# Longer runs for the weights of a fused attention and MLP kernel, strided columns of the first weights, and another order of steps

## The chip, the cores and the metric

The kernel runs on one core of one Trainium2 chip. The metric is the device time of one execution in microseconds. The core has five engines that run side by side, each through its own queue and in order: TensorE (PE, with its weight loads as PEld), VectorE (DVE), ScalarE (ACT), GpSimd (POOL) and SyncE (SP), which here only issues DMAs. 16 DMA engines move data between HBM and the on-chip memory (SBUF). Matmuls write to PSUM, a second on-chip memory.

## The reference, cut to what matters

A gated recurrent attention over 4 sequences of 768 steps, with 8 heads of 48, is followed by a two-layer MLP on its output.

```python
# q, k, v, alpha: (4, 8, 768, 48), alpha in 0.8 to 1.0
for t in range(768):
    state = alpha[:, :, t, :, None] * state + einsum('bhd,bhe->bhde', k[:, :, t], v[:, :, t])
    y[:, :, t] = einsum('bhd,bhde->bhe', q[:, :, t], state)
x = y.transpose(0, 2, 1, 3).reshape(3072, 384)
h = x @ w_in            # w_in (384, 2048)
out = (h * cos(h)) @ w_out   # w_out (2048, 384)
```

## The kernel before, in words

The 3072 rows are worked in 12 pairs J of 256 rows, three pairs to a sequence. A partition holds two consecutive steps of a pair (e is 0 or 1), and the pair's 128 partitions form two chunks (c is 0 or 1) of 64 partitions, so a chunk is 128 steps.

For each pair, the steps are these, with their names in the plan. "load a/k/q/v" (L102) issues one DMA of 384 KB from SyncE's queue. "ln" takes the logarithm of alpha on ScalarE (L139). "cums0" and "cums" (L174, L158) sum the logarithms along the chunk with triangular matrices on TensorE. "icp" and "exps" (L189, L194) are exponentials of minus and plus the sums on ScalarE. "sk" and "sq" (L210, L214) multiply k by the first and q by the second, on GpSimd or, where the plan says ":D", on VectorE. "trans" (L251) transposes scaled k and q on TensorE, "evT" (L261) copies them out of PSUM. "scores" (L266) multiplies them, "mask" (L274) applies the causal mask on VectorE. "castv", "vpe", "vev" and "vst" lay out v. "outer", "add", "state" and "decay" carry the state from chunk to chunk: "add" on VectorE, "state" and "decay" on GpSimd. "yT" (L315) forms the attention's output, transposed, and "evy" (L345) copies it to the tile xT.

The MLP of a pair works in four parts u of 512 hidden columns. "m1" (L354) multiplies 4 x 3 tiles of 128 columns of w1, the stationary operand, by xT (256 moving columns). "sin" (L362) computes the cosine on ScalarE as a shifted sine, "gate" (L367) multiplies it by h on VectorE into the tile gsb. "m2" (L375) takes gsb as the stationary operand and w2 as the moving one; it goes through 16 tiles of 128 hidden columns, in four quarters. Quarter u needs the gate u. "evo" and "out" copy the result out of PSUM and store it. "idle" (L410) issues matmuls on a tile of zeros whose result is not used.

ScalarE needs one table of functions for logarithm and exponential and another for the sine; each change of set is a table load.

The order of all steps is written out in PLAN (L431) and IDLE (L499): each step has a number, all steps are sorted by it and issued in this order (L513), so the numbers set only the order in which each engine's queue is filled. From pair 3 on, "mula" multiplies the two alphas of a partition on GpSimd, and "eb" groups exponentials and the next pair's logarithm.

The weights come in eight DMAs from GpSimd's queue, which also turn float32 into bfloat16: four of w1 (load_w1, L120), one for each part u, and four of w2 (load_w2, L126), one for each m2 quarter. w1 is one tile, with a hidden column in its own place (L94). One row of the reference's w_in gives a run of 512 columns, 2048 bytes, to a partition; one row of w_out gives 1536 bytes. A gate (GATES, L99) holds the load of alpha of pair 2, and with it everything behind it on SyncE's queue, until yT of pair 1 is done.

Of the kernel before, what the change touches and what calls it, by code (L numbers as in the profile page):

```python
# [10 lines left out]
BF = mybir.dt.bfloat16  # L11
# [5 lines left out]
def kernel(  # L17
# [10 lines left out]
    nc = tc.nc  # L28
    B, H, S, D = q.shape
    DM, DF = moe_w_in.shape  # L30
    C = 128
# [6 lines left out]
    KT = DM // C  # L38
    NF = DF // C
    FW = 4  # L40
# [50 lines left out]
    for a in range(2):  # L91
        nc.vector.memset(dmask[64 * a : 64 * a + 64, a : a + 1], 1.0)

    w1 = consts.tile([C, KT, DF], BF, tag="w1", name="w1")  # L94
    w2 = consts.tile([C, NF, DM], BF, tag="w2", name="w2")

    a_sb, kqv, cp_sb, icp_sb, qkT_sb, A_sb, c2_sb = {}, {}, {}, {}, {}, {}, {}
# [19 lines left out]

    WQ = FW * C

    def load_w1(u):  # L120
        nc.gpsimd.dma_start(
            out=w1[:, :, u * WQ : (u + 1) * WQ],
            in_=moe_w_in[:, u * WQ : (u + 1) * WQ].rearrange("(kk p) f -> p kk f", p=C),
        )

    def load_w2(u):  # L126
        nc.gpsimd.dma_start(
            out=w2[:, FW * u : FW * (u + 1)],
            in_=moe_w_out[u * WQ : (u + 1) * WQ, :].rearrange("(a p) d -> p a d", p=C),
        )  # L130

    act_now = [None]
# [221 lines left out]
    def mlp1(J, u):  # L354
        h_ps[J, u] = ps.tile([C, FW, T2], FP, tag="h", name="h_ps", bufs=3)
        for f in range(FW):
            ft = u * FW + f
            for kk in range(KT):
                nc.tensor.matmul(h_ps[J, u][:, f, :], w1[:, kk, ft * C : (ft + 1) * C], xT[J][:, kk, :],  # L359
                                 start=(kk == 0), stop=(kk == KT - 1))  # L360

    def cosine(J, u):  # L362
# [47 lines left out]
    def idle(n):  # L410
# [18 lines left out]


    PLAN = {  # L431
# [66 lines left out]
    }  # L498
    IDLE = [(1201, 12), (6413, 16), (11874, 2), (13039, 6), (14889, 9), (17476, 6)]  # L499

    order = []
    for key, line in PLAN.items():
        kind, *rest = key.split()
# [41 lines left out]
```

## Time and profile before

| | |
|---|---|
| median of 3 runs | 186.75 us (186.71 to 187.4) |
| profiled execution | 186.2 us, its span 184.4 us |
| TensorE busy | 177.7 us (96%) |
| VectorE busy | 132.6 us (72%) |
| ScalarE busy | 127.1 us (69%) |
| GpSimd busy | 83.9 us (45%) |
| granted TensorE clock | 1.00 |

Times in the profile are microseconds from the start of the span unless marked ns. A line of a group or of the timeline names the engine, the line of the kernel, the operation, the tile written, the tiles read, the shape and the count; "w" is a weight tile. The chain that ended last is followed back from the last instruction, at each step to what released it. A matmul's duration includes its way through the array, so matmuls overlap and their pace is read from the distance of their starts.

### The profile page before, as it was taken

Reading aid. Unit: us, or ns where it says so; the run is one execution under the profiler, and the core shown is the slowest. Engines: PE = TensorE matmul, PEld = TensorE weight load, DVE = VectorE, ACT = ScalarE, POOL = GpSimd, SP = SyncE. Lnnn points to the kernel's source line nnn. Section 1 sums busy time; section 2 is a strip of 40 time slices with the busy share of each in tenths; the row PEclk is TensorE's granted clock in tenths of the full one; section 3 lists DMA queues with packets and bytes.
Section 4 is the critical chain, followed back from the end, with each engine's and each line's share of the span. In section 5 each row is a group of like instructions: output and inputs, shape, how many; then the busy total and the mean of one; then the engine's idle time right before and its main releaser. Section 6 shows DMA issues by size and latency. Waiting matters only on the chain.

```text
span 184.4 us, 5780 instructions
## 1 busy us (share of the span) xinstructions
PE 177.7 (96%) x2478; PEld 127.1 (69%) x2480; DVE 132.6 (72%) x176; ACT 127.1 (69%) x166; POOL 83.9 (45%) x116
## 2 busy tenths in 40 slices
PE   7999999899999999999999999999999999999993
PEld 2455687565687776876778668676777786787772
DVE  7367673559889799899548986886979769352651
ACT  2572887899889987779787999637945163372720
POOL 5379830297765693943874189492600121000000
PEclk9999999999999999999999999999999999999999
DMA  5999999999999969968968893050420204010212
GB/s 148 261 261 192 187 203 247 237 271 264 257 197 242 310 174 279 226 158 202 301 151 211 202 304 72 0 132 14 116 73 4 60 5 170 4 43 4 85 43 85
DMA packets 60137, 29.47 MB, mean 160 GB/s; under 512 B 51024, under 2 KB 60112, under 8 KB 60112
## 3 DMA queue, kind: packets, MB, share of 16 engines
q1 hardware_dynamic: 56256, 25.86, 57.6%
q0 software_dynamic: 3712, 3.15, 11.1%
q8 instruction: 19, 0.31, 0.7%
q10 hardware_dynamic: 144, 0.10, 0.2%
q14 instruction: 6, 0.05, 0.1%
HBM read 25.17 MB, written 4.72 MB: 162 GB/s over the span
## 4 chain that ended last, share of the span: by engine, by line
PE 76%; ACT 10%; DMA 7%; DVE 2%; issue 1%; SPq 1%; ACTq 0%
PE h_ps L359 29%; PE o_ps L388 27%; DMA a<-in_alpha_dram 7%; PE y_ps L338 5%; PE A_ps L272 3%; PE T_ps L258 3%; PE idle_ps L414 3%; ACT lna L141 2%; DVE gsb L370 2%; PE U_ps L289 2%; ACT c_sb L365 2%; ACT xT L349 2%; PE o_last L382 1%; ACT L136 1%; ACT L365 1%
## 5 line engine op out<-in xcount | busy, mean ns | idle before, releaser
L370 DVE TENSOR_TENSOR gsb<-h_ps,c_sb 128x1024 bf16<-128x1024 f32 x48 | 58.1, 1221 | 24.1 <-ACT c_sb L365 23.2
L365 ACT ACTIVATE c_sb<-h_ps,halfpi 128x1024 bf16<-128x1024 f32 x48 | 53.1, 1115 | 23.5 <-PE h_ps L359 23.1
L359 PE MATMUL h_ps<-xT,w 128*128 128x256 bf16 x576 | 67.6, 273 | 0.6 <-DVE gsb L370 0.3
L388 PE MATMUL o_ps<-w,gsb 128*128 128x384 bf16 x368 | 66.5, 326 | 0.0
L359 PEld LDWEIGHTS <-w 128*128 128x128 bf16 x576 | 55.5, 98 | 9.5 <-issue 0.9
L388 PEld LDWEIGHTS <-gsb 128*128 128x128 bf16 x368 | 34.1, 98 | 20.7 <-issue 0.2
L277 DVE TENSOR_TENSOR A_sb<-A_ps,msk 128x1024 bf16<-128x1024 f32 x24 | 29.0, 1216 | 3.6 <-PE A_ps L272 3.6
L311 POOL TENSOR_TENSOR un<-us,c 128x384 bf16<-128x384 f32 x20 | 16.7, 837 | 30.0 <-DVE us L303 27.4
L212 POOL TENSOR_TENSOR kh<-k,icp 128x384 bf16<-128x384 f32 x22 | 21.8, 1002 | 14.6 <-ACT icp L192 14.6
L216 POOL TENSOR_TENSOR qh<-q,cp 128x384 bf16<-128x384 f32 x16 | 16.6, 1043 | 0.8 <-DMA q<-in_q_dram 0.8
L149 POOL TENSOR_TENSOR a<-a 128x384 f32<-128x384 f32 x9 | 9.0, 1000 | 15.7 <-DMA a<-in_alpha_dram 15.7
L264 DVE COPY qkT<-T_ps 128x1024 bf16<-128x1024 bf16 x18 | 11.8, 680 | 5.0 <-PE T_ps L258 4.8
L414 PE MATMUL idle_ps<-zeros 128*128 128x512 bf16 x49 | 12.9, 412 | 1.4 <-DVE zeros L52 1.2
L349 ACT CAST xT<-y_ps 128x384 bf16<-128x384 f32 x17 | 9.0, 599 | 5.6 <-PE y_ps L338 5.0
L219 POOL CAST vp<-v 128x768 bf16<-128x768 f32 x12 | 10.2, 854 | 5.7 <-DMA v<-in_v_dram 5.7
L141 ACT ACTIVATE lna<-a 128x768 bf16<-128x768 f32 x12 | 10.1, 843 | 3.5 <-DMA a<-in_alpha_dram 3.5
L136 ACT ACT_TABLE_LOAD x9 | 11.5, 1283 | 0.9 <-PEq L529 0.7
L365 ACT ACT_TABLE_LOAD x9 | 11.5, 1283 | 0.2
L303 DVE TENSOR_TENSOR us<-U_ps,un 128x384 f32<-128x384 f32 x16 | 8.7, 550 | 2.7 <-POOL un L311 2.5
L400 ACT COPY o_sb<-o_ps 128x384 f32<-128x384 f32 x11 | 5.2, 476 | 7.2 <-PE o_ps L388 7.2
L414 PEld LDWEIGHTS <-zeros 128*128 128x128 bf16 x51 | 4.8, 105 | 7.3 <-issue 2.2
L264 ACT COPY qkT<-T_ps 128x1024 bf16<-128x1024 bf16 x6 | 6.0, 1014 | 5.3 <-PE T_ps L258 5.1
(70 smaller groups left out, 159.7 us busy)
## 6 DMA issues: line engine op xcount, KB each, us to landing
a<-in_alpha_dram SPq DMA_DIRECT2D x12, 384.0 KB, 5.9
q<-in_q_dram SPq DMA_DIRECT2D x12, 384.0 KB, 5.7
k<-in_k_dram SPq DMA_DIRECT2D x12, 384.0 KB, 5.9
v<-in_v_dram SPq DMA_DIRECT2D x12, 384.0 KB, 5.6
out_dram<-o_sb SPq DMA_DIRECT2D x23, 192.0 KB, 3.0
vs<-vp SPq DMA_DIRECT2D x36, 64.0 KB, 2.9
w<-in_moe_w_in_dram POOLq DMA_DIRECT2D x4, 384.0 KB, 7.6
w<-in_moe_w_out_dram POOLq DMA_DIRECT2D x4, 384.0 KB, 9.2
```

The lines of the kernel that those rows point to most:

```text
L136: nc.scalar.preload_act_table_set("natural_log_exp_and_others")
L141: nc.scalar.activation(out=lna_t[J % NL][:, :, :, 0:D].rearrange("p e h d -> p h e d"), in_=a_sb.pop(J), func=AF.Ln)
L212: eng.tensor_tensor(out=kh_t[J % NQ][:, e, :, 0:D], in0=kqv["k", J][:, :, e], in1=icp_, op=ALU.mult)
L216: eng.tensor_tensor(out=qh_t[J % NQ][:, e, :, 0:D], in0=kqv["q", J][:, :, e], in1=cp, op=ALU.mult)
L264: copy(out=qkT_sb[J][:, c], in_=T_ps[J][:, c].rearrange("r n e s -> r n (e s)"))
L277: nc.vector.tensor_tensor(out=A_sb[J][:, c].rearrange("s a p t -> s (a p) t"), in0=A_ps.pop((J, c)).rearrange("s a p t -> s (a p) t"), in1 ...
L311: nc.gpsimd.tensor_tensor(out=u, in0=U_sum.pop(n), in1=c2_sb[J][:, :, c].unsqueeze(3).to_broadcast([C, NP, 2, D]), op=ALU.mult)
L359: nc.tensor.matmul(h_ps[J, u][:, f, :], w1[:, kk, ft * C : (ft + 1) * C], xT[J][:, kk, :], start=(kk == 0), stop=(kk == KT - 1))
L365: nc.scalar.activation(out=c_sb[J, u], in_=h_ps[J, u], func=AF.Sin, bias=halfpi, scale=1.0)
L370: nc.vector.tensor_tensor(out=gsb[J][:, u * FW : (u + 1) * FW], in0=h_ps.pop((J, u)), in1=c_sb.pop((J, u)), op=ALU.mult)
L388: nc.tensor.matmul(o_ps[J, c][:, 0:DM], gsb[J][:, ft, c * C : (c + 1) * C], w2[:, ft], start=(ft == 0), stop=(ft == NF - 1))
L414: nc.tensor.matmul(idle_ps[0], zeros[:, 0:C], zeros, start=True, stop=True)
```

## The change

load_w1 loads w1 in two halves of 1024 columns, into two tiles, instead of four quarters into one; a run is now 4096 bytes. The plan still names four w1 steps, and the latter two issue nothing. load_w2 gives partition p the four rows 4p to 4p + 3 of its 512, which lie side by side in HBM, so a run is 6144 bytes instead of 1536. So that hidden units meet their rows of w2, m1 takes for its tile f every fourth column of its part, starting at f: its stationary operand is read with a step of four elements. Parts 0 and 1 read the first half, parts 2 and 3 the second.

The plan is written anew. In the first pairs k is loaded before q; all four multiplies of pairs 0 and 1 are on VectorE, as are three of pairs 2 and 3, while some of later pairs go to GpSimd. Transposes of pair 0 come before the sums of pair 1. yT of pair 1 comes before one m1 step of pair 0 that it followed, and one more m1 step comes before the sums of pair 2. There are 44 idle matmuls instead of 51 (the trace lacks the records of two).

```diff
-    w1 = consts.tile([C, KT, DF], BF, tag="w1", name="w1")
+    w1 = [consts.tile([C, KT, DF // 2], BF, tag=f"w1{r}", name="w1") for r in range(2)]
...
     def load_w1(u):
-        nc.gpsimd.dma_start(
-            out=w1[:, :, u * WQ : (u + 1) * WQ],
-            in_=moe_w_in[:, u * WQ : (u + 1) * WQ].rearrange("(kk p) f -> p kk f", p=C),
-        )
+        if u < 2:
+            cols = slice(2 * u * WQ, 2 * (u + 1) * WQ)
+            nc.gpsimd.dma_start(out=w1[u], in_=moe_w_in[:, cols].rearrange("(kk p) f -> p kk f", p=C))
 
     def load_w2(u):
         nc.gpsimd.dma_start(
             out=w2[:, FW * u : FW * (u + 1)],
-            in_=moe_w_out[u * WQ : (u + 1) * WQ, :].rearrange("(a p) d -> p a d", p=C),
+            in_=moe_w_out[u * WQ : (u + 1) * WQ, :].rearrange("(p a) d -> p a d", a=FW),
         )
...
     def mlp1(J, u):
         h_ps[J, u] = ps.tile([C, FW, T2], FP, tag="h", name="h_ps", bufs=3)
         for f in range(FW):
-            ft = u * FW + f
             for kk in range(KT):
-                nc.tensor.matmul(h_ps[J, u][:, f, :], w1[:, kk, ft * C : (ft + 1) * C], xT[J][:, kk, :],
+                cols = w1[u // 2][:, kk, u % 2 * WQ : (u % 2 + 1) * WQ].rearrange("p (c a) -> p a c", a=FW)[:, f]
+                nc.tensor.matmul(h_ps[J, u][:, f, :], cols, xT[J][:, kk, :],
                                  start=(kk == 0), stop=(kk == KT - 1))
...
-        "load a": "750 2460 26667 27237 34276 40276 44776 46276 52716 68776 86352 100342",
-        "load k": "1890 5250 27807 35776 43276 47776 57976 67354 78979 81849 88912 99772",
-        "load q": "1320 6750 28377 37276 38776 53776 56976 65644 85782 100912 102772 118966",
+        "load a": "750 2925 23850 24420 29562 38429 41429 54304 58004 59504 61004 98634",
+        "load k": "1320 5925 24990 35429 42929 52129 53269 69404 85374 87209 91709 97494",
+        "load q": "1890 7425 32429 36929 45929 52699 63204 70544 84804 90209 98064 122712",
...
-        "w1": "13130 11430 15880 12280",
-        "w2": "19161 17541 20961 22950",
+        "w1": "11430 12280 61723 18603",
+        "w2": "17753 18774 22228 23078",
...
-        "sk 0": "7660 12315:D 38060 42828 55804 60330 73792 86828 93082 113472 119784 131130",
-        "sk 1": "8044:D 13980 36686 43778 54854 64134 78239 85878 98692 112522 114422 129239",
-        "sq 0": "8990:D 15585:D 39010 44194:D 53904 63184 76519 90402 107172 109842 111572 130860:D",
-        "sq 1": "7195:D 14930 38586:D 44728 50458 61464 73876:D 91352 99642 108122 120734 133328:D",
+        "sk 0": "6655:D 12570:D 35664:D 41679:D 49164 66689 71695 88096 91244 103860 108817 133261",
+        "sk 1": "8110:D 13356:D 36402:D 42057 54844 59053 70575 84223 96414 110890 121175 134211",
+        "sq 0": "8560:D 14256:D 39614 43164 53114 67639 77304 86123 92194 104980 123075 129811",
+        "sq 1": "7660:D 13806:D 38664 44114 52164 60003 78254 89229:D 97364 108751:D 112610 130761",
...
-        "trans": "11010 16998 41264 46764 59426 70546 81348 92810 110566 118352 127816 139612",
+        "trans": "9275 14876 41473 45204 57118 68891 79693 91456 108911 116997 125603 138052",
...
-        "yT": "19113 25797 50008 58700 73174 90548 91338 109680 125310 140186 151156 163372",
+        "yT": "18276 22980 46827 56393 71520 88893 89683 108026 123655 138627 149597 160495",
...
-        "m1 0": "22636 29318 53346 64652 77964 96022 98958 113776 129917 147108 155394 166216",
-        "m1 1": "20948 36274 52028 65970 75328 94704 93386 122590 134256 148426 160642 170812",
+        "m1 0": "21429 28072 51691 62998 76309 94667 97303 112775 128357 145548 156458 164657",
+        "m1 1": "20111 31349 50073 64316 73673 93349 92031 121589 132697 146866 159082 167946",
...
-    IDLE = [(1201, 12), (6413, 16), (11874, 2), (13039, 6), (14889, 9), (17476, 6)]
+    IDLE = [(1201, 12), (6413, 12), (9753, 1), (10479, 5), (13514, 6), (15354, 5), (16679, 1), (17666, 2)]
```

106 rows, old and new, of the table PLAN are left out of this document.

## The prediction

> **What bounds the kernel now.** I read the page's engine shares first, then the chain that ended last in order of time, then the timeline of TensorE and its weight loads, then the answers on single engines and the windows of DMA.
>
> The page's first part, its groups and its DMA queues (engine, busy us, share, count; line engine op names shapes xcount | busy, mean ns | idle; queue: packets, MB, share):
>
> ```profile
> PE 177.7 (96%) x2478; PEld 127.1 (69%) x2480; DVE 132.6 (72%) x176; ACT 127.1 (69%) x166; POOL 83.9 (45%) x116
> ...
> L359 PE MATMUL h_ps<-xT,w 128*128 128x256 bf16 x576 | 67.6, 273 | 0.6 <-DVE gsb L370 0.3
> ...
> L359 PEld LDWEIGHTS <-w 128*128 128x128 bf16 x576 | 55.5, 98 | 9.5 <-issue 0.9
> ...
> q1 hardware_dynamic: 56256, 25.86, 57.6%
> q0 software_dynamic: 3712, 3.15, 11.1%
> ```
>
> TensorE is the bound nearly everywhere, so the end is its work plus the time in which it stands or turns over filler matmuls. Those places are near the start, as the chain shows (start us, us, what):
>
> ```profile
> 17.99 1.08 PE idle_ps L414 x5
> ...
> 20.19 1.05 ACT xT L349 x2
> 21.24 0.04 issue
> 21.28 1.47 PE h_ps L359 x12
> ...
> 25.76 0.93 PE y_ps L338 x55
> 26.69 0.02 issue
> 26.71 6.89 DMA a<-in_alpha_dram
> 33.60 0.02 issue
> 33.62 0.85 ACT lna L141
> 34.47 0.04 issue
> 34.52 0.81 PE cums_h L155 x4
> ```
>
> Real work starts at 21.28 with m1 of pair 0. The alpha of pair 2 takes 6.89 us from issue to landing, behind the weights on the DMA engines, and TensorE waits for it: its last m2 matmul before is issued at 33.37 and takes 0.16 of its time, so the sums could start at 33.54 and start at 34.52, 0.98 later. From 37.6 on the chain is TensorE, but for a stretch of ScalarE and VectorE from 102.5 to 119.5.
>
> How fast weights can be loaded (timeline: start, us, engine line, xcount):
>
> ```profile
> 10.43 0.41 PEld L167 LDWEIGHTS <-lna 128*128 128x128 bf16 x8
> 10.59 0.34 PE L167 MATMUL cums_h<-inchunk,lna 128*128 128x2 bf16 x8
> ...
> 52.00 5.24 PEld L359 LDWEIGHTS <-w 128*128 128x128 bf16 x48
> 52.12 5.40 PE L359 MATMUL h_ps<-xT,w 128*128 128x256 bf16 x48
> ```
>
> Eight full weight loads with two-column matmuls: one matmul lasts 0.164, so they follow each other every (0.34 - 0.164)/7 = 25 ns. In m1 the pace is (5.40 - 0.27)/47 = 109 ns, set by 256 moving columns; the load needs at most 25 of these 109.
>
> VectorE and GpSimd on the same scaling (ns min/median/max; timeline):
>
> ```profile
> L212 POOL TENSOR_TENSOR kh<-k,icp x22: 992/1002/1012, 7.9 to 133.0; 128x384 bf16<-128x384 f32 x22
> L212 DVE TENSOR_TENSOR kh<-k,icp x2: 548/892/1236, 8.1 to 12.2; 128x384 bf16<-128x384 f32 x2
> ...
> 12.15 0.55 DVE L212 TENSOR_TENSOR kh<-k,icp 128x384 bf16<-128x384 f32 x1
> ```
>
> The 1236 ns one ran beside GpSimd's kh at 7.94; alone it is 0.55 against GpSimd's 1.00.
>
> **The change part by part.** All against the profiled execution, 184.4 of span in 186.2; the median 186.75 is 0.55 above that run.
>
> *First pairs on VectorE, and the order up to the first m1.* k is loaded before q; loads land about 1.5 apart (384 KB at the window's 260 GB/s), so k lands at 6.0 and q at 7.5. Pair 0's four multiplies run on VectorE, 4 x 0.55, as exponentials arrive between 6.9 and 8.1: done at 9.25 (now 9.82), and pair 0's transposes go ahead of pair 1's sums, at 9.35 instead of 10.87. ScalarE then sets the pace: ln of pair 1 ends at 9.89 as now, two evictions of 1.01 and four exponentials of 0.49 follow, ending near 14.0. VectorE evicts vs at 12.05 (0.55), does four multiplies, the last ending at 14.8; behind them in its queue add 0.56, mask 1.22, add 0.55, mask 1.22: 18.35. yT of pair 0 reads that mask and starts at 18.4, now 19.33. Same evictions after it: first m1 at 20.35, **-0.93**. GpSimd loses three multiplies here and two of four w1 issues (0.8 each), so nothing waits behind them; it is nearly idle from 13 to 15, so the multiplies have no neighbour. The filler falls from 51 to 44 matmuls, which is the same waiting filled.
>
> *yT of pair 1 moves ahead of one m1 step.* Its inputs are ready by 22 (mask of pair 1 ends at 18.35 + 1.22 + 0.55 + 1.21 = 21.3). Small holes around it today (0.2 at 22.7, 0.3 at 26.6, 0.1 at 28.1) become about 0.4 in all: **-0.2**.
>
> *Runs of weights, and the wait for alpha of pair 2.* 3712 packets of queue 0 (11.1% of 16 x 184.4) took 88 ns each and moved 848 bytes, cast from 1696; queue 1's 30 ns for 460. Per packet that is 9 ns plus 0.047 ns a byte read. After: 768 packets of 4096 and 512 of 6144 bytes read, by that line 200 and 296 ns: 305 us of engine time instead of 327, 7% of the 16.4 us that the weights occupy (14.0 to 30.4, between the inputs' packets in the trace's packet records): -1.1. The trace's packet records give 98 ns at 2048 read and 79 at 1536, a steeper saving: 22 + 0.037 a byte, 262 us, -2.6. Lower end: nothing, if a packet costs by bytes alone. I take -1.9, between the two fits. Alpha of pair 2, issued after yT of pair 1 at about 24, lands at 33.6 - 1.9 = 31.7. Pair 2's sums are now behind one more m1 (1.31): TensorE comes to them at 33.6, and needs alpha by 33.6 - 0.05 - 0.85 = 32.7. So the 0.98 between matmuls there shrinks to 0.1: **-0.9**. Cover of 1.0; without it (no DMA gain) the 0.9 comes back. First w1: m1 now needs a half, not a quarter. At worst it lands where the second quarter does now (w1 is 1536 x 98 of 1536 x 98 + 2048 x 79, 0.48 of the 16.4: 7.9 for four quarters, 3.9 for two, from 14.0, plus 1.6 to landing: 19.5), before 20.35.
>
> *What is late next.* TensorE reaches the second m2 quarter of pair 1 5.9 after pair 2's sums start, at 39.55 (four m2 quarters 2.6, sums 1.0 and 0.35, m1 1.31, m2 0.65). It needs a gate that follows four exponentials, ln, a table load 1.28, Sin 1.11 and the gate 1.22: 40.25. New wait **+0.7**. The rest to 52, reordered: **-0.1**.
>
> *Columns read four apart.* 576 weight loads. No row has strided weights. Below: no gain, since the 256 columns set the 109. Above: if all 98 ns of a load's record were serial and stretched as ScalarE's strided xT write stretches against its plain copy (599 to 476, 1.26), 123 + 11 = 134 ns, 25 x 576 = +14.4. I take 0: the nearest row, 25 ns in a window of 109, could be 4 times as long and stay hidden.
> The Trainium skill (SBUF — State Buffer, Door 1, note on cachelines) lets a reader stride free while two reads hit each 16-byte line, up to 8 bf16; 4 is inside, which would leave the sum as it is; no run here shows it. It also (TensorE: Matmul & The Clock Gate, LDWEIGHTS) has 128 columns take 107 ns, which the 25 ns contradict; were strided loads to fall to that estimate, they would just fit into 109.
>
> *Later pairs.* 13 instead of 10 multiplies on VectorE, the rest off TensorE's path; the order from pair 4 on is nearly the old one, moved earlier as a whole, and input DMAs move with it.
>
> Sum: -0.93 - 0.2 - 0.9 + 0.7 - 0.1 = -1.4. Span 183.0, profiled time 184.8, on the median's footing 185.3.
>
> **Rivals.**
> *Strided weights slow m1 (slower).* Place: 576 loads; 0.58 us for each ns over 109; it decides from 1.4/0.576 = 2.4 ns. For it: no row shows such a load, and each load starts only when the matmul before it starts, 11 ns short of the window's end with its 98. Against: 25 ns of streaming. At half the upper end's excess, 121 ns, it adds 7.2 to the forecast: 192.5; at the end 200.
> *The longer runs are not faster.* Alpha lands at 33.6; the 0.9 returns, and its 0.1: gain 0.5, time 186.2. Against: both packet fits.
> *VectorE and GpSimd block each other in pair 2.* Three multiplies of pairs 2 and 3 move to VectorE beside GpSimd's alpha product and decay; 0.7 late each (1236 against 548) would put pair 2's transposes 0.7 late: gain 0.7, time 186.05. For it: that row. Against: GpSimd's own queue has room, and m2 lies ahead of the transposes.
> The Trainium skill (SBUF — State Buffer, Who interferes with whom) states this rule, a VectorE instruction with two SBUF inputs locking against GpSimd's reads; the 1236 ns agree.
>
> **How the numbers follow.** Forecast 0.62 (184.2 to 186.0 on its own), strided weights 0.19, runs no faster 0.10, blocking 0.07, a wait not foreseen that costs over 2.3 us 0.02. About 0.5%, 0.93 us, is what can be told from no change. Faster 0.62, same 0.17, slower 0.21. The time is the forecast's 185.3. The range 184.2 to 188.2 takes in both middle rivals and strided loads up to 114 ns; about 0.15 of large slowdowns and 0.04 below are left out.
>
> **What would show it.** First m1 near 20.4; alpha of pair 2 landed before 32.7 with no ScalarE gap before TensorE's sums; a pace of 109 in m1 with w1 strided; a hole near 39.6; queue 0 with some 1400 packets. A pace over 111, or TensorE idle for alpha, makes it wrong.

## The result and the profile after

| | before | after |
|---|---|---|
| median, first comparison | 186.98 us (186.71 to 187.4, 4 runs) | 185.42 us (184.99 to 185.63, 4 runs) |
| ratio after to before | | 0.9912 [0.9883, 0.994] |
| median, second comparison | 186.53 us (35 runs) | 185.59 us (12 runs) |
| ratio there | | 0.9961 [0.9938, 0.9985] |
| profiled execution and its span | 186.2, 184.4 | 185.63, 183.9; later 184.77, 183.0 |

The changed kernel is faster by 0.9 to 1.6 us; both intervals lie below 1. Every ratio in this document leaves out executions over 1.5% longer than the shortest of their kernel, which are two of the eight with eight idle matmuls and one of the nine with columns one apart; medians take all executions. The first parts of the page of after, in the same columns as before:

```profile
span 183.9 us, 5771 instructions
PE 177.6 (97%) x2473; PEld 133.3 (73%) x2473; DVE 132.8 (72%) x183; ACT 127.3 (69%) x162; POOL 77.2 (42%) x111
...
q1 hardware_dynamic: 56256, 25.86, 58.0%
q0 software_dynamic: 1376, 3.15, 9.2%
...
L360 PE MATMUL h_ps<-xT,w 128*128 128x256 bf16 x576 | 67.4, 273 | 0.2
L360 PEld LDWEIGHTS <-w 128*128 128x128 bf16 x576 | 62.4, 114 | 3.0 <-DVE gsb L371 0.3
```

Queue 0 has 1376 packets instead of 3712, and their engine time is 9.2% of 16 x 183.9 = 271 us instead of 327. A strided weight load is recorded at 114 ns instead of 98, and the m1 matmuls take what they took. TensorE's share rose because the span fell.

This profile gains only 0.5 us of span, and its first m1 starts at 21.23, as in before (21.28). A second profile of the same program starts it at 20.26 and has a span of 183.0. The difference is there before any of the changed steps. TensorE up to 6.5 us, first in the first profile of after, then in the second (start us, us, engine line operation, count, idle before):

```profile
1.20 5.30 PE L415 MATMUL idle_ps<-zeros 128*128 128x512 bf16 x12 [1.20 <-DVE halfpi L77]
6.29 0.53 PE L156 MATMUL cums_h<-lna,tri 128*128 128x384 bf16 x1
```

```profile
1.20 4.08 PE L415 MATMUL idle_ps<-zeros 128*128 128x512 bf16 x12 [1.20 <-DVE halfpi L77]
5.36 0.32 PE L156 MATMUL cums_h<-lna,tri 128*128 128x384 bf16 x1
```

The same twelve idle matmuls lasted 5.30 us and 4.08 us. At the start the idle matmuls follow each other every 0.427 us, later every 0.215, so the clock starts at half; the trace's clock records first show the full clock at 6.77 us in the first profile and at 3.90 us in the second. The queue is in order, so the sums of pair 0 started at 6.29, though their input was ready at about 5.3. Before's profile had its full clock at 3.92, and a second profile of before had it at 4.02, so the second profile of after is the one to set against them:

| profile | full clock from | first m1 | span |
|---|---|---|---|
| before | 3.92 | 21.28 | 184.4 |
| before, second | 4.02 | 21.24 | 184.7 |
| after | 6.77 | 21.23 | 183.9 |
| after, second | 3.90 | 20.26 | 183.0 |

With a like clock the span fell by 1.4 to 1.7 us. The second profile of after is the shortest of its twelve executions (184.77, median 185.59), so the medians are the surer size. The gain sits in two places. The first m1 starts 1.0 earlier. From there to the first m1 step of pair 1 before takes 7.02 and after 6.55, 0.47 less. The next stretch, to the first m1 step of pair 2, gains nothing: 23.81 and 23.88 in the two profiles of before, 23.77 and 23.89 in those of after. In it TensorE's wait for the sums of pair 2 is gone, and a new wait for a gate has come behind it. From that m1 step of pair 2 (52.12 and 50.70) to the last (174.56 and 172.99) the lead only goes from 1.42 to 1.57.

The chain of the second profile of after, where before had 6.9 us of alpha's DMA (start us, us, what):

```profile
29.60 1.95 PE o_ps L389 x12
31.55 1.31 PE h_ps L360 x12
32.86 0.65 PE o_ps L389 x4
33.51 0.79 PE cums_h L156 x4
...
36.89 1.28 ACT L366
...
38.19 2.12 ACT c_sb L366 x2
```

TensorE now goes from m1 and m2 into the sums without a gap. What TensorE still waits for in that profile (total us, times, longest), and the place of the first of these waits on the timeline:

```profile
PE o_ps L389 <- DVE gsb L371: 1.3, 1, 1.3
PE idle_ps L415 <- DVE halfpi L77: 1.2, 1, 1.2
```

```profile
38.52 0.81 PE L389 MATMUL o_ps<-w,gsb 128*128 128x384 bf16 x4
39.33 2.36 DVE L371 TENSOR_TENSOR gsb<-h_ps,c_sb 128x1024 bf16<-128x1024 f32 x2 [1.18 <-ACT c_sb L366]
...
40.62 1.48 PE L389 MATMUL o_ps<-w,gsb 128*128 128x384 bf16 x8 [1.29 <-DVE gsb L371]
```

The first is the new wait, 1.29 us at 39.3. The second stands at the very start, before and after.

### The profile page after: what moved, and what is told of

The parts are those of the page before. It is cut to its first block, busy times and chain, and to the rows that moved or that the text cites. A ratio compares the mean times of both kernels' runs of the same rounds, so it can differ in the third digit from the quotient of the medians.

```text
span 183.9 us, 5771 instructions
## 1 busy us (share of the span) xinstructions
PE 177.6 (97%) x2473; PEld 133.3 (73%) x2473; DVE 132.8 (72%) x183; ACT 127.3 (69%) x162; POOL 77.2 (42%) x111
## 3 DMA queue, kind: packets, MB, share of 16 engines
q0 software_dynamic: 1376, 3.15, 9.2%
## 4 chain that ended last, share of the span: by engine, by line
PE 88%; ACT 5%; DVE 3%; issue 1%; POOL 0%; ACTq 0%; POOLq 0%
PE h_ps L360 33%; PE o_ps L389 31%; PE idle_ps L415 6%; PE y_ps L339 5%; PE A_ps L273 4%; PE T_ps L259 3%; PE U_ps L290 2%; PE o_last L383 1%; DVE A_sb L278 1%; PE cums_h L156 1%; ACT c_sb L366 1%; ACT lna L142 1%; ACT icp L193 1%; PE cums L156 1%; ACT cp L201 1%
## 5 line engine op out<-in xcount | busy, mean ns | idle before, releaser
L389 PE MATMUL o_ps<-w,gsb 128*128 128x384 bf16 x368 | 67.5, 327 | 1.4 <-DVE gsb L371 1.3
L360 PEld LDWEIGHTS <-w 128*128 128x128 bf16 x576 | 62.4, 114 | 3.0 <-DVE gsb L371 0.3
L213 POOL TENSOR_TENSOR kh<-k,icp 128x384 bf16<-128x384 f32 x17 | 17.2, 1017 | 15.1 <-ACT icp L193 13.7
L217 POOL TENSOR_TENSOR qh<-q,cp 128x384 bf16<-128x384 f32 x18 | 17.9, 1007 | 6.1 <-ACT cp L201 5.9
L415 PE MATMUL idle_ps<-zeros 128*128 128x512 bf16 x44 | 13.4, 449 | 1.2 <-DVE halfpi L77 1.2
L265 ACT COPY qkT<-T_ps 128x1024 bf16<-128x1024 bf16 x10 | 9.9, 1014 | 5.4 <-PE T_ps L259 5.2
L401 DVE COPY o_sb<-o_ps 128x384 f32<-128x384 f32 x13 | 7.2, 555 | 6.3 <-PE o_ps L389 6.3
L350 ACT CAST xT<-y_ps 128x384 bf16<-128x384 f32 x12 | 6.5, 594 | 5.0 <-PE y_ps L339 4.6
```

The costliest lines, as they stand in the source:

```text
L213: eng.tensor_tensor(out=kh_t[J % NQ][:, e, :, 0:D], in0=kqv["k", J][:, :, e], in1=icp_, op=ALU.mult)
L217: eng.tensor_tensor(out=qh_t[J % NQ][:, e, :, 0:D], in0=kqv["q", J][:, :, e], in1=cp, op=ALU.mult)
L360: nc.tensor.matmul(h_ps[J, u][:, f, :], cols, xT[J][:, kk, :], start=(kk == 0), stop=(kk == KT - 1))
L389: nc.tensor.matmul(o_ps[J, c][:, 0:DM], gsb[J][:, ft, c * C : (c + 1) * C], w2[:, ft], start=(ft == 0), stop=(ft == NF - 1))
L401: copy(out=t, in_=o_ps.pop((J, c))[:, 0:DM])
L415: nc.tensor.matmul(idle_ps[0], zeros[:, 0:C], zeros, start=True, stop=True)
```

## The experiments

Each is an edit of the changed kernel. In the plan's rows a value stands for a pair, in the order of pairs.

### The loads and columns alone, under the old order

```diff
-    (the rows of PLAN and IDLE after the change)
+    (the rows of before, with)
+        "w1": "11430 13130 15880 12280",
```

> The changed loads and columns under the old order of steps (pair 0's half of w1 issued first, the other half in the place of the third quarter). Theory of the prediction: alpha of pair 2 lands about 1.0 us earlier than the 33.6 of before, so the 0.98 that TensorE waits for it goes to about 0.2, m1 keeps its 109 ns, and the first m1 stays near 21.3: gain 0.7 to 0.9 us, ratio to the kernel before 0.9955. Rival, only the order matters: ratio 1.000, alpha at 33.6. Rival, strided weight loads cost TensorE time: their price eats the gain, ratio 0.998 or more and an m1 pace above 109.

Measured 187.05 (12 runs) against 186.62, ratio 1.0013 [0.9988, 1.0037]: no gain. Alpha of pair 2 landed at 33.28, and still TensorE waited 0.76 for ln:

```profile
33.38 1.28 ACT L137 ACT_TABLE_LOAD   x1
34.67 0.84 ACT L142 ACTIVATE lna<-a 128x768 bf16<-128x768 f32 x1
...
35.56 0.32 PE L156 MATMUL cums_h<-lna,tri 128*128 128x384 bf16 x1 [0.76 <-ACT lna L142]
```

ScalarE was not waiting for the DMA. It was loading its table, behind the last sine. This profile had a late full clock (7.13), which puts everything from the first m1 on (22.36) about 1.1 later, the table load too. But before, with an early clock, shows the same pair of events:

```profile
32.27 1.28 ACT L136 ACT_TABLE_LOAD   x1
...
33.62 0.84 ACT L141 ACTIVATE lna<-a 128x768 bf16<-128x768 f32 x1
```

The table load ended at 33.55 and alpha landed at 33.60. Two waits ended within 0.05 us, and the trace names the later one. In the second profile of before the distance is 0.11. An earlier alpha alone could gain no more than that there. The 0.7 to 0.9 us that were expected did not come.

### The new order alone, with the old loads and columns

```diff
-        "w1": "11430 12280 61723 18603",
+        "w1": "12280 11430 12282 12281",
```

(load_w1, load_w2, mlp1 and the w1 tile as before.)

> The new order and the scaling on VectorE, with the loads and columns of before (four w1 quarters issued one behind the other in the place of the two halves). Theory: the first m1 is about 0.9 us earlier than before at the same start of the full clock, but alpha of pair 2 lands near 33.6 and TensorE stands about 0.9 for it: gain about 0.5 us, ratio 0.997. Rival, the runs don't matter: ratio as the changed kernel's, 0.991. Rival, strided loads cost: with plain columns it is faster than the changed kernel, 0.988 or less.

Measured 186.23 (12 runs) against 186.62, ratio 0.9979 [0.9956, 1.0001]. The first m1 is at 20.34, as early as with the new loads. Behind it TensorE waits for the weights and then for alpha's ln (timeline):

```profile
33.41 0.81 PE L388 MATMUL o_ps<-w,gsb 128*128 128x384 bf16 x4 [0.47 <-DMA w<-in_moe_w_out_dram]
...
34.52 0.32 PE L155 MATMUL cums_h<-lna,tri 128*128 128x384 bf16 x1 [0.30 <-ACT lna L141]
```

The last w2 quarter landed at 33.36 and alpha at 33.60; after the change they land at 31.3 and 32.6. Further waits come later, 0.6 for transposes that GpSimd's multiply holds up and 0.6 inside an m1 step. This profile is of the longest of the twelve executions (187.58, median 186.23), so these later waits need not stand in the others. The longer runs gain nothing under the old order, and without them the new order starts the sums of pair 2 at 34.52 instead of 33.51, 1.0 later. By time alone the orders with and without the new loads can't be told apart here (0.9979 against 0.9961, intervals overlapping); what the loads add is read from these waits.

### The step of the strided columns: 1, 8 and 16 instead of 4

One apart, with w1's hidden units in the wrong places:

```diff
-                cols = w1[u // 2][:, kk, u % 2 * WQ : (u % 2 + 1) * WQ].rearrange("p (c a) -> p a c", a=FW)[:, f]
+                cols = w1[u // 2][:, kk, u % 2 * WQ : (u % 2 + 1) * WQ][:, f * C : (f + 1) * C]
```

> The changed kernel with m1's columns read side by side and all loads as they are, so that hidden units meet other rows of w2 than they should; the work is the same. Theory: the weight loads' record falls from 114 ns back to 98, m1's pace stays 109, and the time is the changed kernel's within 0.3 us, ratio 0.991. Rival, strided loads cost TensorE time: 576 loads at 1 to 2 ns give 0.6 to 1.2 us back, ratio 0.985 to 0.988.

Eight apart, over a half of w1 (hidden units again in the wrong places, as with sixteen):

```diff
+                cols = w1[u // 2][:, kk].rearrange("p (c a) -> p a c", a=2 * FW)[:, u % 2 * FW + f]
```

> The changed kernel with m1's columns read eight apart over a half of w1, 16 bytes from one to the next; loads as they are, so hidden units meet other rows of w2 than they should. The record of a weight load was 98 ns with columns side by side and 114 four apart, and m1 kept 109. Theory, the extra time goes by the 16-byte lines touched (32 columns: 4 lines, then 16, now 32): about 135 ns, and still 109 a matmul, time as the changed kernel's. Rival: one column a line halves the stream again and m1's pace rises above 109; every ns is 0.58 us, so 120 ns would be 6 us slower, ratio 1.03.

Sixteen apart, which needs w1 in one tile:

```diff
+    w1 = consts.tile([C, KT, DF], BF, tag="w1", name="w1")
...
+            nc.gpsimd.dma_start(out=w1[:, :, cols], in_=moe_w_in[:, cols].rearrange("(kk p) f -> p kk f", p=C))
...
+                cols = w1[:, kk].rearrange("p (c a) -> p a c", a=NF)[:, u * FW + f]
```

> As before, with w1 in one tile and columns read sixteen apart over all of it, 32 bytes from one to the next; m1 needs both halves, so the first m1 waits for the second one's landing at 23.3, some 3 us later than in the changed kernel, and hidden units meet other rows of w2 than they should. Theory of lines: 32 lines as with eight apart, so the same record, about 135 ns, and 109 a matmul; the time is the 2 to 3 us of the later start. Rival, the distance itself counts: the record grows again, to 175 or so, and m1's pace passes 109.

The weight loads of m1 at steps 1, 4, 8 and 16 (ns min/median/max, then from and to in us):

```profile
L360 PEld LDWEIGHTS <-w x576: 95/98/99, 20.8 to 174.8; 128*128 128x128 bf16 x192
```

```profile
L360 PEld LDWEIGHTS <-w x576: 110/113/133, 21.1 to 174.9; 128*128 128x128 bf16 x192
```

```profile
L360 PEld LDWEIGHTS <-w x576: 139/143/173, 20.2 to 174.4; 128*128 128x128 bf16 x192
```

```profile
L360 PEld LDWEIGHTS <-w x576: 139/144/169, 23.1 to 179.7; 128*128 128x128 bf16 x192
```

The medians are 98, 113, 143 and 144 ns. The record grows to a step of 8 and no further. The matmuls do not follow: in all four the starts in m1 stand 108 to 110 ns apart at full clock. From the first m1 to the end, steps 1, 4, 8 take 162.8, 162.6 to 162.7, and 163.0 us. Medians are 186.02 (9 runs, ratio 0.9951 [0.9927, 0.9976]) for step 1 and 185.62 (10 runs, 0.9952 [0.9924, 0.998]) for step 8, against 0.9961 for step 4.

That the record levels off at 8 fits the rule in the Trainium skill (SBUF — State Buffer, Door 1, note on cachelines) by which each access that crosses to a new 16-byte line, 8 bf16, pays a penalty: from a step of 8 on, each element lies in another line. The same note would have a step of 4 free; the record shows 15 ns more at 4 than at 1, so in the load itself it was not free, only hidden.

Step 16 is slower, 190.51 (4 runs, ratio 1.0211 [1.0176, 1.0246]), and not by its stride:

```profile
23.13 4.48 PE L360 MATMUL h_ps<-xT,w 128*128 128x256 bf16 x24 [1.89 <-issue]
```

With one tile the first m1 waited for both halves, the second of which landed at 23.04. In the same 24 matmuls that take 2.78 in after, the clock fell to half from 24.04 to 27.45, and they took 4.48. 1.9 and 1.7 account for 3.6 of the 4.7 us of span; 0.9 more is a later wait inside an m1 step. Against this kernel's profile stands the first of after, whose full clock came as late (6.97 and 6.77).

### Fewer idle matmuls at the start

```diff
-    IDLE = [(1201, 12), (6413, 12), (9753, 1), (10479, 5), (13514, 6), (15354, 5), (16679, 1), (17666, 2)]
+    IDLE = [(1201, 8), (6413, 12), (9753, 1), (10479, 5), (13514, 6), (15354, 5), (16679, 1), (17666, 2)]
```

> The changed kernel with 8 instead of 12 idle matmuls at the start. Theory of the clock: full clock is granted at 3.9 us of the span in one execution and at 6.8 in another; in the late ones 12 idle matmuls of 0.427 us hold pair 0's sums until 6.3, though ln is done at 5.3. With 8 the sums start by 5.5 whatever the clock does; the median falls by 0.4 to 0.9 us, ratio 0.987 to 0.989, and the times spread less. Rival, the idle matmuls are needed to bring the clock up: with 8 it comes up later still and the time grows by 0.5 us or more, ratio 0.994 or above.

```profile
1.20 3.59 PE L415 MATMUL idle_ps<-zeros 128*128 128x512 bf16 x8 [1.20 <-DVE halfpi L77]
5.59 0.48 PE L156 MATMUL cums_h<-lna,tri 128*128 128x384 bf16 x1 [0.81 <-ACT lna L142]
...
7.08 4.18 PE L415 MATMUL idle_ps<-zeros 128*128 128x512 bf16 x12
```

The eight end at 4.79, TensorE stands 0.81 us, and the full clock came only at 10.01: idle matmuls still take 0.35 each on average after 7.08, and the first m1 starts at 22.35. The median is 186.05 (8 runs); the ratio, without the two longest, is 0.9947 [0.9912, 0.9983], not told apart from after. The gain of 0.4 to 0.9 that was expected did not come. This profile is of the longest execution, 188.25; that and 187.87 lie above every execution of the changed kernel (at most 186.82), but so does one of 189.01 with columns one apart, which has no such gap. One profile shows the clock later than any without the gap; it does not show that the gap did it.

Ten in the first place, which leaves no gap:

```diff
+    IDLE = [(1201, 10), (6413, 12), (9753, 1), (10479, 5), (13514, 6), (15354, 5), (16679, 1), (17666, 2)]
```

> The changed kernel with 10 instead of 12 idle matmuls at the start. 10 x 0.427 end at 5.5 at half clock, about when pair 0's ln lets its sums start, so TensorE has no hole before full clock is granted. Theory: full clock comes between 3.9 and 7.3 as with 12, not at 10.0 as with 8, and pair 0's sums start by 5.6 instead of up to 6.3; the median falls by 0.3 to 0.6 us, ratio lower by 0.002 to 0.003. Rival: a hole after 10 still puts the clock off, and the time grows by 0.5 us or more.

The full clock came at 5.46, the sums started at 5.44 and the first m1 at 20.28. Median 185.49 (12 runs, ratio 0.9955 [0.9931, 0.9979]), against 185.59 for the changed kernel beside it, which is not told apart; 0.3 to 0.6 less was expected.

### The changed kernel and the kernel before once more

> The changed kernel once more, beside the variants below, to see its spread and a second profile. Theory: its span is set by when full clock is granted; from the first m1 to the end it takes 162.6 to 162.8 us whenever nothing else is late, and the first m1 comes at 20.35 when full clock is granted before 5 us and later by up to 1.1 when it is granted later. Ratio 0.990 to 0.994. Rival, the first m1 is late for another reason: 21.2 whatever the clock does.

> The kernel before against itself, for a second profile and to see what the measurement makes of no change. Theory of the clock: if full clock is granted after 5 us in this profile, its first m1 comes later than 21.3, by up to 1.1, and its span grows by about as much as alpha of pair 2 does not hide; if it is granted near 4, the span is 184.4 again. Ratio 0.998 to 1.002.

The second profile of after is the one read above: the full clock at 3.90, first m1 at 20.26, span 183.0. The second profile of before had it at 4.02, its first m1 at 21.24 and the wait for ln at 0.9. Its time was 0.9993 [0.9958, 1.0027] of before's.

### The new wait: two m2 quarters exchanged

The second m2 quarter of pair 1, which waits for its gate, changes places with the third.

```diff
-        "m2 0 1": "30043 40072 57693 70119 83840 100592 114093 126398 137304 151135 163351 173847",
-        "m2 0 2": "30696 40725 58346 70772 84493 101985 114746 127051 139352 152528 164004 175806",
+        "m2 0 1": "30043 40725 57693 70119 83840 100592 114093 126398 137304 151135 163351 173847",
+        "m2 0 2": "30696 40072 58346 70772 84493 101985 114746 127051 139352 152528 164004 175806",
```

> The changed kernel with m2's second and third quarter of pair 1's first half exchanged, so that TensorE has the third quarter, whose gate is long done, to do while it waits for the gate of the second near 39.8. Theory: the wait of 1.46 us between those two matmuls shrinks to 0.8 and all that follows comes 0.65 earlier: 0.4 to 0.65 us faster than the changed kernel, ratio lower by 0.002 to 0.0035. Rival, pair 2's transposes or its input loads become the wait: no gain.

```profile
41.56 0.82 PE L389 MATMUL o_ps<-w,gsb 128*128 128x384 bf16 x4 [0.65 <-DVE gsb L371]
...
44.33 0.40 PE L273 MATMUL A_ps<-qkT 48*128 48x128 bf16 x8 [0.28 <-DVE qkT L265]
...
45.41 0.81 PE L389 MATMUL o_ps<-w,gsb 128*128 128x384 bf16 x4 [0.40 <-ACT o_sb L401]
```

The wait falls from 1.29 to 0.65, and two waits appear behind it, 0.28 and 0.40. From the first m1 to the first m1 step of pair 2 it takes 30.32, and so does the first profile of after, whose full clock came as late (6.98 and 6.77): nothing is left. Median 185.82 (12 runs, ratio 0.9971 [0.9949, 0.9992]); the 0.4 to 0.65 that were expected did not come. This profile is of the longest of the twelve executions (186.65) and has one more wait, 0.70 inside an m1 step at 96.4, which no profile of after has.

Both together, the exchange and ten idle matmuls:

> Both edits above in the changed kernel. Theory: they add up, 0.8 to 1.2 us faster than the changed kernel, ratio 0.985 to 0.987. Rival: one of them fails as its own rival says, and the gain is the other's alone.

185.28 (12 runs, ratio 0.9941 [0.9917, 0.9965]). It is the lowest median of that comparison, 0.3 below the changed kernel, but the intervals overlap: no version here is shown to beat the changed kernel, and the 0.8 to 1.2 that were expected did not come. From the first m1 to the first m1 step of pair 2 it takes 30.70 with the exchange and ten idle matmuls, and 30.70 with the ten alone.

### The scaling of the first pairs back on GpSimd

```diff
-        "sk 0": "6655:D 12570:D 35664:D 41679:D 49164 66689 71695 88096 91244 103860 108817 133261",
-        "sk 1": "8110:D 13356:D 36402:D 42057 54844 59053 70575 84223 96414 110890 121175 134211",
+        "sk 0": "6655 12570:D 35664:D 41679:D 49164 66689 71695 88096 91244 103860 108817 133261",
+        "sk 1": "8110:D 13356 36402:D 42057 54844 59053 70575 84223 96414 110890 121175 134211",
...
-        "sq 1": "7660:D 13806:D 38664 44114 52164 60003 78254 89229:D 97364 108751:D 112610 130761",
+        "sq 1": "7660:D 13806 38664 44114 52164 60003 78254 89229:D 97364 108751:D 112610 130761",
```

> The changed kernel with three multiplies of pairs 0 and 1 back on GpSimd, as before the change: first sk of pair 0, second sk and sq of pair 1. Theory: a multiply takes 1.00 on GpSimd instead of 0.55; pair 0's transposes wait little, but pair 1's second sk and sq, one behind the other on GpSimd with two w1 issues ahead, end about 0.9 later, and the first m1 comes 0.3 to 0.9 us later than in the changed kernel at the same start of full clock: ratio higher by 0.002 to 0.005. Rival, the order alone made the earlier first m1: no difference.

```profile
13.05 1.01 POOL L213 TENSOR_TENSOR kh<-k,icp 128x384 bf16<-128x384 f32 x1
14.01 1.34 POOL L217 TENSOR_TENSOR qh<-q,cp 128x384 bf16<-128x384 f32 x1
...
15.41 0.38 PE L259 MATMUL T_ps<-ident_bf,qh 64*128 64x64 bf16 x14 [0.16 <-POOL qh L217]
```

With the full clock at 3.92, the first m1 starts at 20.65 instead of 20.26: the three multiplies on VectorE are worth 0.39 of the 1.0 there. The rest is put down to the order, as the new order with the old loads has its first m1 just as early (20.34). Median 185.73 (9 runs, ratio 0.9938 [0.9914, 0.9963]), not told apart from after.

## Why the prediction was right, and where its steps were off

**The sum.** Forecast: 1.4 less span. Measured with a like clock: 1.4 (against the first profile of before) and 1.7 (against the second). In medians the gain was 1.56 in the first comparison and 0.94 in the second, so the predicted 185.3 lies 0.1 to 0.3 below the two medians of after. The sum came out partly by luck, because errors of opposite sign cancelled. The first profile of before and the second of after give -1.03 for the -0.93 up to the first m1, -0.47 for the -0.2 around yT, and +0.08 for the three terms behind (-0.9, +0.7 and -0.1, together -0.3): 0.37 more gain than forecast, then 0.38 less. The new order with the old loads has both of the first two gains (first m1 at 20.34, then 6.55), and in its one profile loses 1.0 in the third stretch (24.84). By these profiles the longer runs only make up for what the new order would lose there. A kernel with the new order up to pair 1's first m1, and the old loads and order behind it, was not run; by these stretches it could gain as much.

**First m1 at 20.35, -0.93: right.** It stands at 20.26, 1.0 earlier. The steps behind it hold: VectorE's multiplies in place of GpSimd's carry 0.39 of it, and yT of pair 0 starts at 18.30 where 18.4 was forecast. The forecast did not see that this start moves by up to 1.1 us with the moment at which the full clock is granted, and the first profile of after fell on a late one.

**yT of pair 1, -0.2: the stretch gained 0.47, but not by yT.** The 0.2 put down as a hole at 22.7 is work. From before's chain, then TensorE's timeline of the first profile of after:

```profile
21.28 1.47 PE h_ps L359 x12
22.75 0.28 PE vs_ps L234 x2
23.04 2.73 PE h_ps L359 x24
```

```profile
20.79 0.35 PE L235 MATMUL vs_ps<-vp,ident_bf 64*64 64x384 bf16 x2
21.23 2.78 PE L360 MATMUL h_ps<-xT,w 128*128 128x256 bf16 x24
```

Two matmuls of "vpe", which lay out v of pair 1, stood between the first two m1 steps and now stand ahead of the first. Before, the second step starts 1.68 after the first, and after, 1.31: 0.38 of the 0.47. The m1 step ahead of yT and yT together take 2.63 before and after, so moving yT closed nothing. The last 0.08 is the small hole at 28.1. The prediction did not count the move of "vpe".

**Alpha of pair 2, -0.9: the effect right, its cause half wrong.** The wait of TensorE is gone: the sums of pair 2 start 6.21 after pair 1's first m1 step before and 6.68 after, with an m1 step of 1.31 more between, so 0.85 is saved. ScalarE still waits 0.54 for alpha, beside m2. But the step said that the faster weights bring alpha 1.9 earlier and leave a cover of 1.0. Alpha came 1.04 earlier (33.60 to 32.56) and was needed by 32.7: a cover of 0.1. With ten idle matmuls TensorE still waits 0.2 for this ln. That alpha came earlier is the loads' doing: with the old loads in the new order it was issued at 24.18 instead of 26.71 and still landed at 33.60. Engine time of queue 0 did fall as the steeper of the two fits said (327 to 271, the fit 262), by 17%; the last weight landed only 1.2 earlier of 16.4 us, 7%. The step took the packets' time for the engines' time. From 15 to 27 us, with the input loads at rest, the packets fill a share of 1.24 of the 16 engines' time before and 1.10 in the second profile of after. A share over 1 means that packets' records overlap; with longer packets they overlap less, and the rate rose only from 191 to 208 GB/s, 9%. What bounds that rate was not found. And the wait of before had two causes, as the old order with the new loads shows: the table load ended 0.05 before alpha landed. The forecast should have asked what ScalarE would have done with an earlier alpha. The extra m1 step ahead of the sums hides the table load; the loads only keep alpha from being late in the new order.

**The longer runs are not faster: refuted, its price right at its place.** With the old loads in the new order the sums of pair 2 start 1.0 later, the 0.9 and 0.1 of that rival, but half of the wait already stands at the last w2 quarter. The two waits of 0.6 further on were not in its price.

**The gate's wait, +0.7 at 39.55: right place, mis-sized.** It is 1.29 at 39.3 in the second profile. The chain from the sums through four exponentials, ln, table load, sine and gate took 7.1 us instead of the 6.6 put down, and TensorE came 0.2 earlier. That the next waits stand close behind, so that 0.65 taken from it gains nothing, the exchange shows.

**Strided columns, 0: right.** The load's record grew by 15 ns and the pace stayed at 109. The timeline of m1 in after:

```profile
24.95 5.36 PEld L360 LDWEIGHTS <-w 128*128 128x128 bf16 x48
25.16 5.41 PE L360 MATMUL h_ps<-xT,w 128*128 128x256 bf16 x48
```

This is the first profile. (5.41 - 0.27) / 47 = 109 ns, while a load is recorded at 113 ns, longer than the pace: loads overlap. The row that decided, 25 ns per streamed load, was the nearer one. The rival that strided weights slow m1 is refuted even at a step of 8, with a record of 143.

**VectorE and GpSimd blocking in pair 2: refuted.** The two multiplies of pair 2 on VectorE take 0.56 and 0.55 us in the first profile of after, shown here, and 0.80 and 0.55 in the second:

```profile
36.25 1.03 DVE L213 TENSOR_TENSOR kh<-k,icp 128x384 bf16<-128x384 f32 x2 [1.18 <-ACT icp L193]
```

The rule named there (the Trainium skill, SBUF — State Buffer, Who interferes with whom) cost 0.25 once at this place, not 0.7, and TensorE had no wait for these transposes. Of the seven multiplies of k on VectorE in the second profile none is slower than that 0.80. It started at 35.50, while GpSimd's un ran (35.05 to 35.88). Three others overlapped with a computation of GpSimd that started after them, and took 0.55 to 0.56; the 1236 ns of before had started behind GpSimd's kh. In these rows only the one that came second was slow.

## What to carry to other kernels

Before a wait is put down to the DMA that ended last, look what the waiting engine would have done had it come earlier: here a table load ended 0.05 us before, and the faster DMA alone gained nothing. The length of a weight load's record says little about its cost: with 256 moving columns, a record longer than the pace of the matmuls (143 against 109 ns) stayed hidden, and the matmuls' distance is what to read. A wait that is gone is worth only what the next wait leaves: here 0.85 was saved at one place and the stretch around it took as long as before. So measure a forecast's terms from one fixed step of the program to the next, and look what stood in a hole before it is closed. When two profiles of one kernel differ by a microsecond, compare the first moments of the clock before explaining anything behind them.

## What the runs showed of the hardware

The moment at which TensorE gets its full clock varies from execution to execution, from 3.9 to 7.1 us after the start where the work at the start left no gap. As a matmul takes twice as long until then (0.427 against 0.215 us for an idle one), in-order filler that is meant to bridge a wait ends late and holds up the first real work. In the profiles of the new order the first m1 follows it. Left out are the one with multiplies back on GpSimd, the one with eight idle matmuls and the one with w1 in one tile, which have reasons of their own to be late:

| kernel | full clock from | first m1 |
|---|---|---|
| after, second | 3.90 | 20.26 |
| exchange and ten idle | 4.18 | 20.28 |
| new order, old loads | 4.59 | 20.34 |
| eight apart | 5.01 | 20.35 |
| ten idle | 5.46 | 20.28 |
| one apart | 6.25 | 20.96 |
| after | 6.77 | 21.23 |
| exchange | 6.98 | 21.32 |

Up to 5.0 the start of m1 doesn't move (up to 5.5 with ten idle matmuls); at 7.0 it is 1.1 later. The profiled execution of before lay 0.55 us under the median of its runs, and its clock came early, at 3.92; but the second profile of before, with 4.02, lay only 0.1 under its median, so the early clock is not shown to be the reason. Whether the spread of the runs (186.82 - 184.77 = 2.1 us for the changed kernel) comes from the same moment is open: for the other runs only the mean granted clock is on record. A second source shows in three of the fourteen profiles: between 96 and 101 us TensorE stands for 0.62, 0.70 and 0.88 us inside an m1 step (new order with old loads, exchange, sixteen apart), where the trace shows nothing that it waits for.

A clock once granted can be lost again: in the kernel with columns sixteen apart TensorE stood 1.89 us ahead of its first m1, and 0.9 us after the wait ended the clock was at half for 3.4 us. The wait of 1.29 us at 39.3 in the second profile of after has no such drop behind it. Why the one did and the other did not was not tried.

A weight load's record grows with the step of its columns, 98, 113, 143 and 144 ns at 1, 4, 8 and 16 bf16 elements.
